# Block-ordered q columns and normalised tiles in an adaLN block of linear attention and a bilinear FFN

## The chip, the cores and the metric

The kernel runs on one core of one Trainium2 chip. The metric is the device time of one execution in microseconds (us). Before the change it was run three times; the median is 558.22 us (558.07 to 559.64).

## The reference

The input is x (2048 tokens by 512), a condition vector c and weights, all float32. c gives six vectors of 512 (shifts, scales, gates). The block is two steps with residuals:

```
mod = silu(c) @ w_mod                      # sa, ca, ga, sb, cb, gb
h = layernorm(x) * (1 + ca) + sa
q, k, v = split(h @ wqkv)                  # 32 heads of 16
pq, pk = phi(q), phi(k)                    # phi(t) = (t + 1 if t > 0 else exp(t)) + 1e-6
o = pq @ (pk.T @ v) / (pq . sum(pk) + 1e-6)     # per head
x = x + ga * (o @ wo)
h = layernorm(x) * (1 + cb) + sb
x = x + gb * (((h @ w_gate) * (h @ w_up)) @ w_down)   # inner width 1376
```

## The kernel before, in words

**Precision.** Every float32 matrix is split into a high part (a copy rounded to fp32r) and a low part (the rest). A product is three matmuls, high x high, high x low and low x high. In `split` (L195) ScalarE (ACT) makes the high part and VectorE (DVE) or GpSimd (POOL) the low part.

**Tiles.** The 2048 tokens are 16 tiles of 128, in four chunks of four. A buffer is 128 x 512 float32 from one pool of 94; PSUM has four banks of the pool ps_acc and four of ps_w.

**First stage (to about 140 us).** Chunk by chunk tokens are normalised (class `Norm`, `xhat` L256), turned on TensorE (PE) and modulated; k products (`proj`, L304), phi, and the sums of keys times normalised tokens in four banks. In iteration i == 2 of this loop the q weights are split (L517). The q products of tiles 0 to 5 are made in the loop, those of tiles 6 to 15 after it. `zb` (L558) holds the sum of keys for the denominators.

**Second stage (about 140 to 275 us).** `wp` is the product of the key-value sums with wo, four high/low pairs. For each tile phi(q) is divided by its denominator (`den_p`, `den_b`, `den_c`), transposed and multiplied by wp on top of x in PSUM (`y_seed` L740, `y_a` L748); `y_b` (L757) takes the bank back to x, and for the last chunk DVE makes the statistics from the bank. `y_step` (L766) is one tile of this. Tiles 0 to 7 are transposed on PE. Tiles 8 to 15 (FLIPPED) are transposed otherwise: `move_out` writes the tile to DRAM, `move_in` fetches it with 32-row blocks exchanged between partitions, and `turn_v` (L719) lets a DVE transpose turn the 32 x 32 blocks; `turn_h` and `turn_l` make the high and low parts. The DVE transpose reads every fourth word (`"p (m i s) -> p m s i"`), so the row order of what it gives is (partition, k) and not (k, partition); for these tiles a second copy of wp in that order is needed: `wp_store` (L691) writes wp to DRAM, `wp_fetch` (L698) reads it back as `wp4`.

**Third stage (about 265 us to the end).** The FFN's columns are taken in groups of 128 (`fts`). Three groups (`lone`) are done plainly for chunks 0 and 1 (`gate_up`, `down`), beside the second stage. The others go through `block` (L1044), a scheme of seven half products instead of eight over pairs of chunks: the left side (class `Left`) has sums s1 to s4 of the normalised, transposed tokens, the right side (class `Right`, L980) sums t1 to t4 of gate and up weights, each split into high and low. `Right.sums` makes the t, `Right.high` and `Right.lows` the parts; helpers `right_load`, `right_sums`, `right_split` (L1133 to L1144). A block has the points p1, p5, p6, p2, p7, p3, p4; each is six matmuls (`times`, L1021) into one of four banks a, b, c, d, and between them ACT copies banks (`copy`, L1031): after p1 bank a is copied into b, and p6 adds to b. `fill(n)` advances the blocks by n points.

The tokens of chunks 2 and 3 reach the blocks without PE: `stow` (L882) writes the normalised tile to DRAM, `unstow` reads it back, `flip` (L894) is a DVE transpose into `wide`, reading every fourth word, and `flipped` (L899) applies scale and shift on ACT, reading `wide` in runs of 32 words. Their row order is again (partition, k). So the gate and up weights for these chunks are loaded in that order (`wg_4`, `wu_4`), and scale and shift are turned by `by_fours` (L875, four small DMAs through DRAM).

**What sets the order.** The program is a schedule written by hand (`manual_schedule`): each engine executes its instructions in the order in which the code records them, and the code from L1203 on fixes how the second stage, the lone groups and the first block interleave. All DMAs are issued by SyncE (SP), in order. Waits between engines follow from the tiles; a buffer of the pool waits for its last user.

The stretch that the change reorders is L1279 to L1346. Two lines of it:

```
    y_step(14, seed=None)      # L1336: the matmuls of tile 14
    fill(1)                    # L1337: p1 of the first block
```

Of the kernel before, what the change touches and what calls it, by code (L numbers as in the profile page):

```python
# [14 lines left out]
P = 128  # L15
# [9 lines left out]
def tile_adaln_block(  # L25
# [33 lines left out]
    wg_4 = w_gate.rearrange("(p k) f -> p k f", p=P)  # L59
    wu_4 = w_up.rearrange("(p k) f -> p k f", p=P)  # L60
# [152 lines left out]
    def cut(pair, a, b):  # L213
        return pair[0][:, a:b], pair[1][:, a:b]


    class Norm:
        def __init__(self, tiles):
# [37 lines left out]
        def xhat(self, *js):  # L256
            for j in js:
                self.n[j] = B("n")
                nc.scalar.activation(self.n[j], self.tiles[j], AF.Identity,  # L259
                                     scale=self.rstd[:, j:j + 1], bias=self.nmr[:, j:j + 1])  # L260

        def xhat_on(self, engine, *js):
# [238 lines left out]
    for i in range(NT):  # L501
        ch, j = divmod(i, NJ)
        done = 0
        if i > 2:
            ahead[i + 2] = proj(i + 2, wk) if i + 2 < NT else proj(i + 6 - NT, wq)
        if i in q_at:
            qps = proj(q_at[i], wq)
        def turn_x():
            to, *ks = turn_at[i]
            nx.transpose(*ks)  # L510
            nx.modulated(ca, sa, *ks, cast=nc.vector)
            norm[to:] = [nx]
# [24 lines left out]
        if ch + 2 < NCH and j == 3:  # L537
            nx = nx2
            nx.stats(2, 3)
            nx.rstd_of()  # L540
            nx.nmr_of()
            nx.xhat(0, 1)
        if i + 2 < NT:
            k_phi(i + 2, ahead.pop(i + 2))
        else:
            q_a(i + 6 - NT, ahead.pop(i + 2))
            q_b(i + 6 - NT)
        if i in q_at:
            q_a(q_at[i], qps)
            q_b(q_at[i])  # L550
        if i + 1 < NT:
            z_add(i + 1)
        if i == NT - 2:
            pairs["z"] = split_raw(zacc, low=nc.gpsimd)
        if i == NT - 1:
            zps = row_sum(pairs["z"])
            zb = consts.tile([P, D], F32, name="zb")
            nc.scalar.activation(zb, zps, AF.Identity, bias=eps_z)  # L558
        t_tile(i, *range(done, KD))
        if i in extra:  # L560
            extra[i]()
# [4 lines left out]

    pzs = {}
    den0 = consts.tile([P, NH], F32, name="den0")

    def den_z():  # L570

        nc.vector.reduce_sum(den0, zb.rearrange("p (h i) -> p h i", i=DH), axis=AX.X)
        nc.vector.tensor_scalar(den0, den0, EPS_PHI, EPS_DEN, op0=ALU.mult, op1=ALU.add)

    def den_p(ch, *js, on=None):
        for j in js:
            pzs[ch, j] = B("f")
            (on or nc.gpsimd).tensor_tensor(pzs[ch, j], phq[ch * NJ + j], zb, op=ALU.mult)

    def den_r(ch, *js):  # L580
        if ch not in dens:
# [8 lines left out]
            den_r(ch, j)  # L590

    def den_b(ch):
        nc.vector.tensor_tensor(dens[ch], dens[ch], den0.unsqueeze(1).to_broadcast([P, NJ, NH]), op=ALU.add)
        nc.vector.reciprocal(dens[ch], dens[ch])

    def den_c(*tiles):
# [87 lines left out]
        turn_h(i)  # L684
        turn_l(i)

    FLIPPED = range(8, NT)
    SUMS = (0, 1, 2)
    wp4, moved = [], {}

    def wp_store():  # L691
        to = [tc.dram_tile([D, D], F32, name=f"wp_{part}") for part in range(2)]
        for g in range(KD):
            for part in range(2):
                nc.sync.dma_start(to[part][g * P:(g + 1) * P], f32(wp[g][part]))
        wp4.append(to)

    def wp_fetch():  # L698
        rows = [x.rearrange("(p k) d -> p k d", k=KD) for x in wp4.pop()]
        for k in range(KD):  # L700
            wp4.append((B("w", dt=F32R), B("w", dt=F32R)))
            for part in range(2):
                nc.sync.dma_start(f32(wp4[k][part]), rows[part][:, k])

    def move_out(*tiles):

# [12 lines left out]
    def turn_v(i):  # L719

        tps[i] = B("f")
        nc.vector.transpose(tps[i].rearrange("p (s m i) -> p m s i", m=NQ, i=BL),
                            moved.pop(i).rearrange("p (m i s) -> p m s i", m=NQ, i=BL))

    def turned_v(i):
        turn_v(i)
# [21 lines left out]
    def y_a(i):  # L748
        if i not in yps:
            y_seed(i)  # L750
        pq = pqs.pop(i)
        for k in range(KD):
            (ah, al), (bh, bl) = cut(pq, k * P, (k + 1) * P), (wp4 if i in FLIPPED else wp)[k]
            for x, y in ((ah, bh), (ah, bl), (al, bh)):
                nc.tensor.matmul(yps[i], x, y, start=False, stop=k == KD - 1 and x is al, skip_group_check=True)  # L755

# [115 lines left out]
        norm2[ch].nmr_of()  # L872
        ln2_xhat(ch)

    def by_fours(col, name):  # L875

        t, v = consts.tile([P, KD], F32, name=name), tc.dram_tile([D], F32, name=name + "_row")
        nc.sync.dma_start(v.rearrange("(k p) -> p k", p=P), col)
        nc.sync.dma_start(t, v.rearrange("(p k) -> p k", k=KD))
        return t  # L880

    def stow(ch, *js):  # L882

        for j in js:
# [9 lines left out]
    def flip(ch, *js):  # L894
        for j in js:
            nc.vector.transpose(wide[:, j].rearrange("p (m s i) -> p m s i", m=NQ, i=BL),
                                blocks.pop((ch, j)).rearrange("p (m i s) -> p m s i", m=NQ, i=BL))

    def flipped(ch, *ks):  # L899
        for k in ks:  # L900
            f = B("f")
            nc.scalar.activation(f.rearrange("p (x i) -> p x i", i=BL),
                                 wide.rearrange("p j (m s i) -> p (j m) s i", m=NQ, i=BL)[:, :, k],
                                 AF.Identity, scale=cb4[:, k:k + 1], bias=sb4[:, k:k + 1])
            blocks[ch, "f", k] = f

    stowed, blocks = {}, {}
# [8 lines left out]
    cb4, sb4 = by_fours(cb, "cb4"), by_fours(sb, "sb4")  # L916
    for ch in range(NCH):
        norm2[ch] = Norm(xts[ch])

# [60 lines left out]
    class Right:  # L980


        def __init__(self, f, plain):
            f0, self.n = fts[f]
            self.up, self.low = self.tile("raw"), self.tile("raw")
            for t, kh in ((self.up, 0), (self.low, 1)):
                for i, v in enumerate((wg_v, wu_v) if plain else (wg_4, wu_4)):
                    nc.sync.dma_start(t[:, i], v[:, kh * KH:(kh + 1) * KH, f0:f0 + self.n])

        def tile(self, tag, dt=F32):  # L990
# [141 lines left out]

    def right_load(n):  # L1133
        if n < len(steps):
            rights[n] = Right(steps[n][1], steps[n][0][0] in PLAIN)

    def right_sums(n, on=None):
        if n < len(steps):
# [74 lines left out]
    y_step(0, lambda: den_c(3), lambda: q_b(11))  # L1213
    y_step(1)
    y_step(2, lambda: split_gu(f0, nc.gpsimd))
    y_step(3, lambda: scale_down(f0), wp_store, turn=False, seed=False)
    ps12 = proj(12, wq)
    y_b(3)
    norm2[0].rstd_of()
# [36 lines left out]
    den_c(7)  # L1256
    den_a(2, 2, on=nc.vector)
    g()
    y_step(5, lambda: den_a(2, 3, on=nc.vector), wp_fetch)
# [37 lines left out]
    y_banks += [acc_bank(), acc_bank()]  # L1297
    y_seed(12, y_bank)
    norm2[2].nmr_of()
    norm2[2].xhat(0, 1)  # L1300
    turn_l(12)
    first[0].sum("s1", "s3", on=nc.gpsimd)
    g(lambda: turn_v(13))
    y_seed(13, y_bank)
    norm2[2].xhat(2, 3)
    turn_h(13)
    turn_l(13)
    move_in(14, 15)
# [40 lines left out]
    norm2[3].nmr_of()  # L1349
    unstow(2)  # L1350
    fill(1)
    norm2[3].xhat(0)
    fill(1)
    norm2[3].xhat(1)
    fill(1)
    norm2[3].xhat(2)
    stow(3, 0, 1)
    fill(1)
    norm2[3].xhat(3)
    stow(3, 2)  # L1360
    second = [Left((2, 3), k) for k in range(KH)]

# [52 lines left out]
```

## Time and profile before

| what | value |
|---|---|
| median of three runs | 558.22 us (558.07 to 559.64) |
| the profiled execution | 559.39 us |
| its span, first to last instruction | 557.7 us |
| mean granted TensorE clock | 0.997 |
| POOL busy | 203.0 us (36%) |
| mean DMA rate | 108 GB/s |

The profile is of one execution. A page gives busy shares, the chain of work that ended last, and groups of instructions by line, with count, busy time, mean time of one, idle time ahead of them and what ended it. In the timeline each row has start, duration, engine, line, operation, output and inputs; a bracket gives idle time of the engine before it and who ended it. PE is matmul, PEld weight loading. The end of a matmul in the rows is modelled, and consecutive matmuls overlap in them; the distance between starts gives the pace.

### The profile page before, as it was taken

The page shows a single profiled execution, that of the slowest core. Times are in us where ns is not written, and L with a number is a line of the kernel's source. Part 1 is how long each engine was busy: PE and PEld are TensorE (multiplying, and loading weights), DVE is VectorE, ACT ScalarE, POOL GpSimd, SP SyncE. Part 2 cuts the span into 40 slices and gives each one's busy share as a digit, 9 for nine tenths or more (in the row PEclk, how much of TensorE's full clock was granted, in tenths as well). Part 3 has the DMA queues.
Part 4 walks back from the last instruction along what each step waited for, and adds up shares of the span by engine and source line. Part 5 has one row for each costly group of instructions (what it writes and reads, how often), then busy time and mean ns, then how long its engine had stood idle before and what let it go on. Part 6 is the DMA issues. An engine that isn't in the chain of part 4 may idle for free.

```text
span 557.7 us, 7356 instructions
## 1 busy us (share of the span) xinstructions
PE 550.1 (99%) x2505; PEld 451.3 (81%) x2505; DVE 377.8 (68%) x605; ACT 291.4 (52%) x539; POOL 203.0 (36%) x203
## 2 busy tenths in 40 slices
PE   8999999999999999999899999999999999999997
PEld 6888888888888878878688888887888888888886
DVE  7896968977947886877877587886553544434435
ACT  3695856646477567566683545554444444444110
POOL 2000000101012300055698666566667446446200
PEclk9899999999999999999999999999999999999999
DMA  8900203220532605846435162591335222100004
GB/s 279 384 16 2 75 25 103 101 76 1 155 100 92 188 20 169 264 143 162 132 75 148 42 201 65 188 318 29 113 114 150 59 56 58 56 21 0 1 0 150
DMA packets 59141, 60.39 MB, mean 108 GB/s; under 512 B 8608, under 2 KB 37536, under 8 KB 59104
## 3 DMA queue, kind: packets, MB, share of 16 engines
q1 hardware_dynamic: 59104, 59.93, 34.3%
q8 instruction: 19, 0.31, 0.2%
q14 instruction: 18, 0.15, 0.1%
HBM read 43.65 MB, written 16.26 MB: 107 GB/s over the span
## 4 chain that ended last, share of the span: by engine, by line
PE 92%; DVE 3%; ACT 2%; DMA 1%; issue 1%; SPq 0%; DVEq 0%; ACTq 0%
PE bank L1026 32%; PE acc L1106 6%; PE acc L1107 6%; PE acc L1108 6%; PE acc L755 5%; PE bank L209 5%; PE bank L211 5%; PE bank L210 5%; PE acc L351 3%; PE acc L349 3%; PE acc L350 3%; PE bank L839 2%; PE bank L837 2%; PE bank L838 2%; PE bank L272 2%; DMA x<-in_A_x_dram 1%
## 5 line engine op out<-in xcount | busy, mean ns | idle before, releaser
L1026 PE MATMUL bank<-h,w 128*128 128x512 f32 (+1 forms) x798 | 185.4, 390 | 1.5 <-ACT bank L1031 1.5
L1026 PEld LDWEIGHTS bank<-h,w 128*128 128x128 f32 (+1 forms) x798 | 148.1, 186 | 35.8 <-ACT bank L1031 2.6
L1031 ACT ACTIVATE bank<-bank 128x512 f32<-128x512 f32 (+1 forms) x38 | 22.1, 583 | 137.1 <-PE bank L1026 137.0
L824 DVE TENSOR_TENSOR x<-acc,x 128x512 f32<-128x512 f32 (+1 forms) x73 | 48.4, 681 | 47.4 <-PE acc L1108 47.3
L1012 POOL TENSOR_TENSOR w<-raw,w 128x256 fp32r<-128x256 f32 (+3 forms) x38 | 41.3, 1086 | 95.2 <-ACT w L1005 95.2
L1107 PE MATMUL acc<-w,kh 128*128 128x512 f32 (+2 forms) x154 | 59.6, 387 | 0.0
L1106 PE MATMUL acc<-w,kh 128*128 128x512 f32 (+2 forms) x154 | 59.6, 387 | 0.0
L1108 PE MATMUL acc<-w,kl 128*128 128x512 f32 (+2 forms) x154 | 59.5, 386 | 0.0
L197 POOL TENSOR_TENSOR w<-raw,w 128x512 fp32r<-128x512 f32 (+1 forms) x25 | 36.0, 1442 | 55.3 <-ACT w L196 28.5
L250 POOL TENSOR_TENSOR rstd<-ve,half 128x4 f32<-128x4 f32 (+1 forms) x10 | 10.8, 1080 | 120.7 <-DVE ve L249 68.0
L1012 POOL TENSOR_TENSOR w<-t,w 128x512 fp32r<-128x512 f32 (+1 forms) x38 | 49.3, 1320 | 0.0
L197 DVE TENSOR_TENSOR kl<-u,kh 128x512 fp32r<-128x512 f32 (+1 forms) x38 | 26.4, 733 | 30.2 <-ACT kh L196 30.2
L209 PE MATMUL bank<-w,h 128*128 128x512 f32 x104 | 40.8, 392 | 0.0
L211 PE MATMUL bank<-w,h 128*128 128x512 f32 x104 | 40.5, 390 | 0.0
L210 PE MATMUL bank<-w,h 128*128 128x512 f32 x104 | 40.5, 389 | 0.0
L755 PE MATMUL acc<-w,xh 128*128 128x512 f32 x120 | 37.7, 395 | 0.0
L1106 PEld LDWEIGHTS acc<-w,kh 128*128 128x128 f32 (+1 forms) x154 | 28.9, 188 | 6.0
L1108 PEld LDWEIGHTS acc<-w,kl 128*128 128x128 f32 (+1 forms) x154 | 28.9, 188 | 5.9
L1107 PEld LDWEIGHTS acc<-w,kh 128*128 128x128 f32 (+1 forms) x154 | 28.9, 188 | 5.9
L1085 DVE TENSOR_TENSOR u<-bank,u 128x512 f32<-128x512 f32 (+1 forms) x19 | 13.1, 687 | 28.9 <-PE bank L1026 22.9
L259 ACT ACTIVATE n<-x,nmr,rstd 128x512 f32<-128x512 f32 x30 | 22.9, 804 | 12.2 <-DVE nmr L254 12.2
L196 ACT ACTIVATE w<-raw 128x512 fp32r<-128x512 f32 (+2 forms) x44 | 26.3, 619 | 1.9 <-DVE raw L804 1.0
(206 smaller groups left out, 1125.1 us busy)
## 6 DMA issues: line engine op xcount, KB each, us to landing
raw<-in_w_mod_dram SPq DMA_DIRECT2D x24, 256.0 KB, 3.8
raw<-in_B_w_down_dram SPq DMA_DIRECT2D x20, 256.0 KB, 3.2
raw<-in_B_w_gate_dram SPq DMA_DIRECT2D x36, 128.0 KB, 3.7
raw<-in_B_w_up_dram SPq DMA_DIRECT2D x36, 128.0 KB, 3.6
x<-in_A_x_dram SPq DMA_DIRECT2D x16, 256.0 KB, 5.7
out_dram<-x SPq DMA_DIRECT2D x15, 256.0 KB, 2.6
raw<-in_A_wqkv_dram SPq DMA_DIRECT2D x12, 256.0 KB, 5.4
wp<-w SPq DMA_DIRECT2D x8, 256.0 KB, 3.3
```

Of the source, the lines that this page charges most:

```text
L196: nc.scalar.activation(h, src, AF.Copy)
L197: (low or nc.vector).tensor_tensor(l, src, f32(h), op=ALU.subtract)
L209: nc.tensor.matmul(ps, ah, bh, start=i == 0, stop=False)
L210: nc.tensor.matmul(ps, ah, bl, start=False, stop=False)
L211: nc.tensor.matmul(ps, al, bh, start=False, stop=i == n - 1)
L755: nc.tensor.matmul(yps[i], x, y, start=False, stop=k == KD - 1 and x is al, skip_group_check=True)
L824: nc.vector.tensor_tensor(xt[:, a:b], dn[j][:, a:b], xt[:, a:b], op=ALU.add)
L1012: sub = lambda out, x, y: (on or nc.gpsimd).tensor_tensor(out, x, f32(y), op=ALU.subtract)
L1026: mm = lambda x, y, **kw: nc.tensor.matmul(ps, x[:, k], y, skip_group_check=True, **kw)
L1106: nc.tensor.matmul(ps, hh[:, a:b], dh[:n, c:d], start=i == 0, stop=False)
L1107: nc.tensor.matmul(ps, hh[:, a:b], dl[:n, c:d], start=False, stop=False)
L1108: nc.tensor.matmul(ps, hl[:, a:b], dh[:n, c:d], start=False, stop=i == len(hs) - 1)
```

## The change

The DVE transposes for tiles 8 to 15 and for chunks 2 and 3 now read contiguous runs. For this the columns inside each row are put into block order before: column (s, q, i), with s of 4, q of 4 and i of 32, stands at place (q, s, i). What the transposes give is then in the plain row order (k, partition). It follows that:

- q weights are split into block order; q products of tiles 0 to 7 read them back in row order, those of tiles 8 to 15 come out in block order. Denominators of tiles 8 to 15 use a copy of zb and of den0 in block order.
- The normalised tiles of chunks 2 and 3 are written in block order.
- wp_store, wp_fetch, wp4, by_fours, wg_4 and wu_4 go.
- Beside that, the order at the start of the first block changes: right_sums(0), right_split(0), turn_v(15) with its parts, the splits s3 and right_sums(1) stand earlier, the additions of down(1, (2, 3)) later, and the banks are no longer permuted.

PE executes the same instructions in the same order, as the two programs show. On POOL one copy is added, on DVE one small copy, and on SP 20 DMAs go.

```
+    FLIPPED = range(8, NCH * NJ)
+    def by_block(x):
+        return x.rearrange("p (s q i) -> p q s i", q=NQ, i=BL)
+    def by_row(x):
+        return x.rearrange("p (q s i) -> p s q i", q=NQ, i=BL)
+    def split_blocks(raw):
+        h, l = B("w", dt=F32R), B("w", dt=F32R)
+        view = lambda x: x.rearrange("p (q s i) -> p q s i", q=NQ, i=BL)
+        nc.scalar.activation(view(h), by_block(raw), AF.Copy)
+        nc.vector.tensor_tensor(view(l), by_block(raw), view(f32(h)), op=ALU.subtract)
+        return h, l
...
+        def xhat_blocks(self, *js):
+            for j in js:
+                self.n[j] = B("n")
+                nc.scalar.activation(self.n[j].rearrange("p (q s i) -> p s q i", q=NQ, i=BL),
+                                     self.tiles[j].rearrange("p (s q i) -> p s q i", q=NQ, i=BL), AF.Identity,
...
-        product(ps, [(cut(norm[ch].t[k], j * P, (j + 1) * P), w[k]) for k in range(KD)])
+        rows = w is wq and i not in FLIPPED
+        product(ps.rearrange("p (s q i) -> p s q i", q=NQ, i=BL) if rows else ps,
+                [(cut(norm[ch].t[k], j * P, (j + 1) * P), tuple(by_row(x) for x in w[k]) if rows else w[k])
+                 for k in range(KD)])
...
-            wq.extend(split_raw(r) for r in raw_q)
+            wq.extend(split_blocks(r) for r in raw_q)
...
+            zq = B("z")
+            nc.gpsimd.tensor_copy(zq.rearrange("p (q s i) -> p q s i", q=NQ, i=BL), by_block(zb))
...
+        nc.vector.tensor_copy(den0q.rearrange("p (q s h) -> p q s h", q=NQ, s=KD),
+                              den0.rearrange("p (s q h) -> p q s h", q=NQ, s=KD))
...
         nc.vector.transpose(tps[i].rearrange("p (s m i) -> p m s i", m=NQ, i=BL),
-                            moved.pop(i).rearrange("p (m i s) -> p m s i", m=NQ, i=BL))
+                            moved.pop(i).rearrange("p (m s i) -> p m s i", m=NQ, i=BL))
...
-            (ah, al), (bh, bl) = cut(pq, k * P, (k + 1) * P), (wp4 if i in FLIPPED else wp)[k]
+            (ah, al), (bh, bl) = cut(pq, k * P, (k + 1) * P), wp[k]
...
             nc.vector.transpose(wide[:, j].rearrange("p (m s i) -> p m s i", m=NQ, i=BL),
-                                blocks.pop((ch, j)).rearrange("p (m i s) -> p m s i", m=NQ, i=BL))
+                                blocks.pop((ch, j)).rearrange("p (m s i) -> p m s i", m=NQ, i=BL))
...
-                for i, v in enumerate((wg_v, wu_v) if plain else (wg_4, wu_4)):
+                for i, v in enumerate((wg_v, wu_v)):
...
     g()
+    right_sums(0, nc.vector)
     y_step(11, lambda: move_in(12), turn=False, seed=False)
...
     turn_v(14)
-    take = down(1, (2, 3))
+    down_13 = down(1, (2, 3))
     first[1].sum("s1", "s3", "s2", "s4", on=nc.gpsimd)
+    right_split(0)
     y_seed(14, y_bank)
     turn_h(14)
+    turn_v(15)
+    turn_l(14)
+    turn_h(15)
     first[0].split("s1", "s2")
-    turn_l(14)
+    first[1].split("s1", "s2")
     y_b(13)
+    turn_l(15)
+    for x in first:
+        x.split("s3")
+    right_sums(1, nc.vector)
     y_seed(15, y_bank)
-    right_sums(0, nc.vector)
-    take()
-    first[1].split("s1", "s2")
-    turn_v(15)
     for n in range(4):
         banks.append(bank())
-    banks[:] = [banks[n] for n in (2, 0, 1, 3)]
     turn_bank[0] = acc_bank
-    right_split(0)
     draw_load(0)
...
     y_step(14, seed=None)
     fill(1)
     y_b(14)
-    right_sums(1, nc.vector)
-    first[0].split("s3", "s4")
     fill(1)
-    first[1].split("s3", "s4")
+    for x in first:
+        x.split("s4")
     fill(2)
+    down_13()
     y_step(15)
```

More of the change, by code (lines that the diff above doesn't have):

```diff
@@ L259, in xhat @@
                 nc.scalar.activation(self.n[j], self.tiles[j], AF.Identity,
+                                     scale=self.rstd[:, j:j + 1], bias=self.nmr[:, j:j + 1])
+        def xhat_blocks(self, *js):
[3 more added lines that the diff above has]
+                                     self.tiles[j].rearrange("p (s q i) -> p s q i", q=NQ, i=BL), AF.Identity,
                                      scale=self.rstd[:, j:j + 1], bias=self.nmr[:, j:j + 1])
@@ L568, in tile_adaln_block @@
     den0 = consts.tile([P, NH], F32, name="den0")
+    den0q = consts.tile([P, NH], F32, name="den0q")
     def den_z():
@@ L577, in den_p @@
             pzs[ch, j] = B("f")
[L578 removed]
+            (on or nc.gpsimd).tensor_tensor(pzs[ch, j], phq[ch * NJ + j], zq if ch * NJ + j in FLIPPED else zb, op=ALU.mult)
     def den_r(ch, *js):
@@ L592, in den_b @@
     def den_b(ch):
-        nc.vector.tensor_tensor(dens[ch], dens[ch], den0.unsqueeze(1).to_broadcast([P, NJ, NH]), op=ALU.add)
+        nc.vector.tensor_tensor(dens[ch], dens[ch], (den0q if ch * NJ in FLIPPED else den0).unsqueeze(1).to_broadcast([P, NJ, NH]), op=ALU.add)
         nc.vector.reciprocal(dens[ch], dens[ch])
@@ L685, in turn @@
         turn_l(i)
-    FLIPPED = range(8, NT)
     SUMS = (0, 1, 2)
[L689 to L703, printed above, removed]
+    moved = {}
     def move_out(*tiles):
@@ L873, in ln2_nx @@
         ln2_xhat(ch)
[L875 to L880, printed above, removed]
     def stow(ch, *js):
@@ L980, in tile_adaln_block, with __init__ @@
     class Right:
-        def __init__(self, f, plain):
+        def __init__(self, f):
             f0, self.n = fts[f]
@@ L1134, in right_load @@
         if n < len(steps):
-            rights[n] = Right(steps[n][1], steps[n][0][0] in PLAIN)
+            rights[n] = Right(steps[n][1])
     def right_sums(n, on=None):
@@ L1215, in tile_adaln_block @@
     y_step(2, lambda: split_gu(f0, nc.gpsimd))
-    y_step(3, lambda: scale_down(f0), wp_store, turn=False, seed=False)
+    y_step(3, lambda: scale_down(f0), turn=False, seed=False)
     ps12 = proj(12, wq)
@@ L1258, in tile_adaln_block @@
     g()
-    y_step(5, lambda: den_a(2, 3, on=nc.vector), wp_fetch)
+    y_step(5, lambda: den_a(2, 3, on=nc.vector))
     y_step(6, lambda: den_b(2), lambda: ready(8))
@@ L1299, in tile_adaln_block @@
     norm2[2].nmr_of()
-    norm2[2].xhat(0, 1)
+    norm2[2].xhat_blocks(0, 1)
     turn_l(12)
@@ L1304, in tile_adaln_block @@
     y_seed(13, y_bank)
-    norm2[2].xhat(2, 3)
+    norm2[2].xhat_blocks(2, 3)
     turn_h(13)
@@ L1351, in tile_adaln_block @@
     fill(1)
-    norm2[3].xhat(0)
+    norm2[3].xhat_blocks(0)
     fill(1)
-    norm2[3].xhat(1)
+    norm2[3].xhat_blocks(1)
     fill(1)
-    norm2[3].xhat(2)
+    norm2[3].xhat_blocks(2)
     stow(3, 0, 1)
     fill(1)
-    norm2[3].xhat(3)
+    norm2[3].xhat_blocks(3)
     stow(3, 2)
```

5 lines of the change are left out of this document (1 added, 4 removed).

## The prediction

> **What bounds the kernel now.** I read the page first, then the waits of TensorE (PE), then the chain in order of time, then the timeline around the one wait that counts.
>
> ```profile
> span 557.7 us, 7356 instructions
> PE 550.1 (99%) x2505; PEld 451.3 (81%) x2505; DVE 377.8 (68%) x605; ACT 291.4 (52%) x539; POOL 203.0 (36%) x203
> PE 92%; DVE 3%; ACT 2%; DMA 1%; issue 1%; SPq 0%; DVEq 0%; ACTq 0%
> ```
>
> PE is busy 99% of the span, and 92% of the chain that ended last is PE. So an edit on another engine pays only where PE waits for it, and an edit to the matmuls themselves pays or costs directly. The waits of PE say where it waits:
>
> ```profile
> PE acc L148 <- DVE w L143: 2.0, 1, 2.0
> PE bank L1026 <- ACT bank L1031: 1.5, 1, 1.5
> PE bank L279 <- ACT n L259: 0.4, 1, 0.4
> ```
>
> The first and third belong to the start, which the change doesn't touch. The second is one wait of a block's matmuls (L1026) for a PSUM copy on ACT (L1031). The next rows show its place; the first of them, from the chain, gives PE's undisturbed pace: 9.52 us for 42 matmuls of 512 columns, 0.2267 us each.
>
> ```profile
> 302.69 9.52 PE bank L1026 x42
> ```
>
> ```profile
> 260.86 0.62 PE L755 MATMUL acc<-w,xh 128*128 128x512 f32 x2
> ...
> 263.59 3.19 PE L1026 MATMUL bank<-h,w 128*128 128x512 f32 x12
> 263.70 2.38 DVE L197 TENSOR_TENSOR h<-s,h 128x512 fp32r<-128x512 f32 x2
> 263.73 3.50 POOL L1012 TENSOR_TENSOR w<-t,w 128x512 fp32r<-128x512 f32 x2
> ...
> 266.00 1.08 DVE L722 STREAM_TRANSPOSE f<-u 128x512 f32<-128x512 f32 x1
> 267.12 0.63 ACT L676 ACTIVATE xh<-f 128x512 fp32r<-128x512 f32 x1 [2.61 <-DVE f L722]
> 267.19 1.27 POOL L1012 TENSOR_TENSOR w<-raw,w 128x512 fp32r<-128x512 f32 x1
> 267.66 0.58 ACT L1031 ACTIVATE bank<-bank 128x512 f32<-128x512 f32 x1
> ...
> 268.29 3.02 PE L1026 MATMUL bank<-h,w 128*128 128x512 f32 x12 [1.51 <-ACT bank L1031]
> ...
> 271.15 0.61 PE L755 MATMUL acc<-w,xh 128*128 128x512 f32 x2
> ```
>
> Twelve matmuls from 263.59 (the points p1 and p5 of the first block) would let the next (p6) start at 263.59 + 12 x 0.2267 = 266.31. It starts at 268.29, 1.98 us late. The next twelve should lead to 271.01 and lead to 271.15, 0.14 late. That is **2.1 us** of PE time. Its cause reads backwards: p6 adds into bank b, which ACT copies from bank a (267.66). ACT runs in order, and ahead of the copy stands the high part of tile 15 (L676), which waited 2.61 us for the DVE transpose turn_v(15) (L722, 266.00), which stood behind two low parts of left sums (L197) that took 2.38 us while POOL made the low parts of the first right side.
>
> **The change part by part.** (a) *Order.* PE's instructions keep their order exactly; what moves is on DVE and ACT. right_sums(0), four DVE subtractions, goes ahead of norm2[2].rstd_of.
>
> ```profile
> 240.54 0.69 DVE L197 TENSOR_TENSOR kl<-phi,kh 128x512 fp32r<-128x512 f32 x1 [0.70 <-ACT kh L196]
> 243.35 0.17 DVE L247 TENSOR_SCALAR ve<-sums 128x4 f32<-128x4 f32 x1 [2.11 <-ACT acc L238]
> ```
>
> ```profile
> 230.67 0.40 SPq L988 DMA_DIRECT2D raw<-in_B_w_up_dram  x1
> raw<-in_B_w_up_dram SPq DMA_DIRECT2D x36, 128.0 KB, 3.6
> ```
>
> ```profile
> 261.06 0.39 DVE L994 TENSOR_TENSOR t<-raw 128x256 f32<-128x256 f32 x1
> 262.17 0.42 DVE L994 TENSOR_TENSOR t<-raw,t 128x256 f32<-128x256 f32 x1
> ```
>
> They took 261.06 to 262.59, 1.53 us, and now stand in a hole of 2.11 us between 241.23 and 243.35. Their weights were asked for by 230.67 and land about 3.6 us later, so the new wait on them is over before DVE gets there; if it were not, L247 and the normalisation of chunk 2 would queue behind it.
>
> right_split(0) follows the copy of y 12 on ACT, so POOL can make the low parts as soon as its eight left sums are done; turn_v(15) and its high part now precede all left splits, and four left splits move ahead of y_b(13). I lay the new order out from old rows:
>
> ```profile
> 255.21 0.68 DVE L229 BATCH_NORM_STATS2 st<-acc 128x6 f32<-128x512 f32 x1
> 255.32 1.29 POOL L944 TENSOR_TENSOR s<-f,s 128x512 f32<-128x512 f32 x1
> 256.10 1.10 DVE L722 STREAM_TRANSPOSE f<-u 128x512 f32<-128x512 f32 x1
> 260.96 0.60 ACT L746 ACTIVATE acc<-x 128x512 f32<-128x512 f32 x1 [1.57 <-DVE st L229]
> ```
>
> ```profile
> L1012 POOL TENSOR_TENSOR w<-raw,w 128x256 fp32r<-128x256 f32 x18 | 14.5, 804 | 90.2 <-ACT w L1005 90.2
> ```
>
> DVE is at turn_v(14) at 256.10 as before and, at the old 1.10 each, through turn_v(15) at 258.3. Then come five subtractions (xl of 14, four left lows), the statistics of y 13, seed 15 on ACT (which reuses that bank), and the copy of a into b. POOL has its last sum done at 256.6 and four lows to make, one of half size: 0.80 + 3 x 1.27 = 4.6 us, to 261.2 if alone. ACT makes the high parts and copies y 13 from 258.3 on (five of 0.63, to 261.5, then the copy to 262.1). Without contention DVE's five (0.69 each) follow ACT and end at 262.2. If DVE and POOL took strict turns, DVE's 3.45 and the 2.9 that POOL has left at 258.3 add up to 6.35, to 264.7. The statistics (0.68) then end between 262.9 and 265.4, seed 15 (0.60) between 263.5 and 266.0. The copy (0.58) can't start before p1's last matmul ends: its start 263.59 + 5 x 0.2267 = 264.72, plus 0.39 for one (the 390 ns of L1026 below), 265.1. So the copy ends between 265.7 and 266.6, due at 266.31. I take it as in time: the two L197 beside POOL took 2.38 in place of 1.38, 0.5 more each, and about three of the five meet POOL, so they end at 258.3 + 3.45 + 1.5 = 263.3 and seed 15 at 264.6. The other bound is 0.3 late, plus 0.14 for the restart.
>
> ```profile
> L1026 PE MATMUL bank<-h,w 128*128 128x512 f32 x756 | 175.6, 390 | 1.5 <-ACT bank L1031 1.5
> L680 DVE TENSOR_TENSOR xl<-f,xh 128x512 fp32r<-128x512 f32 x8 | 7.7, 965 | 4.3 <-ACT xh L676 4.1
> L680 DVE TENSOR_TENSOR xl<-bank,xh 128x512 fp32r<-128x512 f32 x8 | 5.5, 688 | 4.2 <-ACT xh L676 4.2
> ```
>
> The same subtraction takes 688 ns with one input in PSUM and 965 with both in SBUF, where POOL works beside it. The Trainium skill, SBUF — State Buffer, section "Who interferes with whom", says that a DVE instruction with two SBUF inputs and a reading GpSimd instruction hold one lock, and the loser blocks fully; these two rows agree. By that rule the strict turns, with 0.4 us of the gain lost, would be the end; it is part of the first rival.
>
> The second left parts' other moves have room: with p6 at 266.31 the third point that needs s3 and t3 (p7) comes after two more groups of six and the twelve of tile 15, at 266.31 + 24 x 0.2267 = 271.75; s3's lows and right_sums(1) (1.53) follow the statistics on DVE and are through by about 268.5. The adds of down_13 (two of 0.68) move behind them; nobody takes those two banks before the first down_group. SP's draw_load(1) now waits for POOL's last right low and delays right_load(2) by some 2 us; these weights are used a block later.
>
> (b) *Contiguous flips.* Sixteen DVE transposes read runs instead of every fourth word.
>
> ```profile
> L722 DVE STREAM_TRANSPOSE f<-u 128x512 f32<-128x512 f32 x8 | 8.8, 1097 | 0.0
> L896 DVE STREAM_TRANSPOSE wide<-u 128x512 f32<-128x512 f32 x8 | 8.6, 1088 | 0.0
> L902 ACT ACTIVATE f<-wide,sb,cb 128x512 f32<-128x512 f32 x8 | 6.4, 806 | 0.7 <-DVE wide L896 0.7
> L259 ACT ACTIVATE n<-x,nmr,rstd 128x512 f32<-128x512 f32 x30 | 22.9, 804 | 12.2 <-DVE nmr L254 12.2
> ```
>
> They would fall from about 1.09 us towards the 0.69 of a plain DVE pass, at most 0.4 each; two of them lie in the chain above, but the layout already holds with 1.10, so I book nothing. The flips of chunks 2 and 3 lie beside blocks with DVE less than full. xhat_blocks and split_blocks use runs of 32 words on ACT or DVE: L902 reads just such runs and takes 806 ns against 804 for the contiguous L259, so I price them at nothing; at the most 0.4 us a DVE pass (the price of L722's words).
>
> ```profile
> 40.13 2.49 DVE L197 TENSOR_TENSOR w<-raw,w 128x512 fp32r<-128x512 f32 x4
> 44.25 0.39 PE L209 MATMUL bank<-w,h 128*128 128x512 f32 x1
> 132.02 2.49 DVE L197 TENSOR_TENSOR w<-n,w 128x512 fp32r<-128x512 f32 x4
> 135.07 0.22 PE L209 MATMUL bank<-w,w 128*128 128x128 f32 x1
> ```
>
> Four split lows end at 42.6 and PE first reads wq at 44.25: 1.6 us of cover, just what 4 x 0.4 would use. The added zq copy (POOL, about one 1.29 us pass) and den0q (a 128x32 DVE pass, 0.2) delay DVE's w<-n by at most 1.5 us; they end at 134.5, PE starts on them at 135.07 with the first and needs the last later: covered within about 0.1 us.
>
> (c) *PE reads q weights by rows.* For tiles 0 to 7, 8 x 12 = 96 matmuls read their moving side in 16 runs of 32 words. PE writes the same contiguous bank. No matmul of this trace does that. Nearest rows: L902, the same runs on another engine, +2 ns; L722, words instead of runs, 1097 against 688, x1.6, which would be 0.136 us each, 13 us in all. I take nothing, because L902 has the same geometry; below nothing is excluded, since the same number of columns passes. The Trainium skill, Advanced Engine Details and Errata, section "Memory Cachelines", says that SBUF reads within one 16-byte line go at full rate, which these runs satisfy, but also, of PSUM, that non-contiguous patterns slow matmuls; no run yet shows which holds here.
>
> (d) *Removed.* Sixteen 256 KB transfers of wp and four column transfers leave SP. PE waits for none of them, so nothing.
>
> **Sum:** -2.1 (stall), 0 for the rest: the profiled execution of 559.39 us (span 557.7 and 1.7 around it) would be 557.3. It lies 0.2% over the median of the runs; the median 558.22 less 2.1 is 556.1, and I forecast **556.2**, 0.1 being left for an incomplete restart.
>
> **The rivals.** *A new wait takes part of the old one's place*: seed 15 and the copy come late, by strict turns of DVE and POOL (0.4 us: 556.5 to 556.6; 10%), or because tile 15's block or a sum arrives later than laid out (up to all 2.1 us: 558.2; 14%). For it: a copy that starts at 265.1 has only 0.6 us to spare. Against: seed 15 has 0.5 us in front of that start.
>
> *PE reads runs slower* (the other side): place, the 96 matmuls of (c). At 21 ns each (9%) the gain is used up, at 39 ns the kernel is slower by 0.3%; at L722's ratio it ends at 556.1 + 13 = 569. For it: 128-byte hops are new to PE, which has no slack at all. Against: L902. 18%, with the smaller mishaps of that side.
>
> That the flips don't become faster (the price being that of writing runs) changes nothing here, as the layout used 1.10.
>
> **How the numbers follow.** 0.3% of 558.22 is 1.67 us, about what a measurement can tell from no change. Forecast 58%: 555.6 to 556.5, faster. First rival 10% + 14% = 24%: 556.5 to 558.2, within 0.3%. Second rival 18%: from 558.4 up to 569; the range takes the first two whole and the edge of the third: 555.5 to 558.5. Faster 0.58, same 0.24, slower 0.18.
>
> **What would show it.** Right: no PE wait on the bank copy, the block's first 24 matmuls without a break, and all later times 2 us earlier. Transposes near 0.7 us confirm (b).
>
> ```profile
> 155.65 2.75 PE acc L755 x12
> ```
>
> If the q products of tiles 0 to 7 take more than 0.227 us a matmul, so that tile 0's output product (L755) starts later than 155.65, (c) is wrong. If PE waits at p6 again, look whether DVE's statistics or POOL's lows ended last.

## The result and the profile after

The changed kernel takes 557.41 us (median of 10 runs, 557.13 to 558.21); the kernel before, run beside it, 558.76 us (10 runs, 558.07 to 561.21). The ratio is 0.9967, 95% interval 0.9952 to 0.9982: 1.8 us faster by the ratio (1.0 to 2.7), 1.35 by the medians. The ratio compares means, and four of the ten runs of the kernel before took 559.64 to 561.21 us, which the median hardly feels. The profiled execution took 557.53 us. In later runs, on other occasions, the same kernel gave 557.33 us against 558.9, ratio 0.9966 (0.9954 to 0.9978).

The page of the changed kernel, the same lines as those shown of before (span, busy time, chain by engine):

```profile
span 555.8 us, 7319 instructions
PE 549.9 (99%) x2505; PEld 451.2 (81%) x2505; DVE 371.4 (67%) x606; ACT 291.4 (52%) x539; POOL 204.1 (37%) x204
PE 99%; DVE 0%; issue 0%
```

PE was 92% of the chain before and is 99% of it now: ahead of the first block the old chain ran over ACT, DVE and a transfer from 238 to 268 us, and the new one stays on PE. Its waits (engine, line waited at, releaser: total us, times, longest):

```profile
PE acc L146 <- DVE w L141: 2.0, 1, 2.0
```

The wait on the bank copy is gone; the 2.0 us at the start, which the change doesn't touch, are left. (The small wait of 0.4 us at the start is absent from this execution and there again in the next one of the same kernel.) The timeline shows the place of the old stall:

```profile
255.81 1.31 DVE L736 STREAM_TRANSPOSE f<-u 128x512 f32<-128x512 f32 x2
...
257.54 3.45 POOL L1018 TENSOR_TENSOR w<-t,w 128x512 fp32r<-128x512 f32 x2
...
258.34 5.50 DVE L195 TENSOR_TENSOR h<-s,h 128x512 fp32r<-128x512 f32 x4 [0.21 <-ACT h L194]
...
260.95 1.73 POOL L1018 TENSOR_TENSOR w<-raw,w 128x512 fp32r<-128x512 f32 x1
...
263.69 5.60 PE L1032 MATMUL bank<-h,w 128*128 128x512 f32 x24
263.76 0.69 DVE L242 BATCH_NORM_STATS2 st<-acc 128x6 f32<-128x512 f32 x1
...
264.48 0.60 ACT L760 ACTIVATE acc<-x 128x512 f32<-128x512 f32 x1 [3.09 <-DVE st L242]
...
265.25 0.58 ACT L1037 ACTIVATE bank<-bank 128x512 f32<-128x512 f32 x1 [0.17 <-PE bank L1032]
```

Before, there were two rows of 12 matmuls with 1.51 us of idle time between; now the block's first 24 matmuls are one row. Both transposes are through by 257.1, and the copy starts at 265.25 behind PE itself (0.17 us of ACT idle, ended by p1's last matmul), no longer behind ACT's high part of tile 15.

The groups of the transposes, and of the operations that now write or read in block order (count, busy us, mean ns):

```profile
L736 DVE STREAM_TRANSPOSE f<-u 128x512 f32<-128x512 f32 x8 | 5.5, 700 | 0.0
L903 DVE STREAM_TRANSPOSE wide<-u 128x512 f32<-128x512 f32 x8 | 5.5, 699 | 0.0
L279 ACT ACTIVATE n<-x,nmr,rstd 128x512 f32<-128x512 f32 x8 | 6.2, 804 | 0.0
L225 ACT ACTIVATE w<-raw 128x512 fp32r<-128x512 f32 x4 | 2.2, 626 | 0.0
```

The transposes fall from 1097 and 1088 ns to 700 and 699. The block-ordered normalisation (L279, 804) costs what the plain one did, the block-ordered high part of the q weights (L225, 626) what a plain one does.

What came back is on PE. One q product, tile 0, in the view of a line's matmuls: L209 of the kernel before, then L207 of the changed one. One line issues every third matmul of the twelve; the columns are duration min/median/max in ns and the first and last start.

```profile
L209 PE MATMUL bank<-w,h x4: 389/389/389, 44.2 to 46.3; 128*128 128x512 f32 x4
```

```profile
L207 PE MATMUL bank<-w,h x4: 395/396/396, 43.6 to 45.7; 128*128 128x512 f32 x4
```

The modelled duration follows the pace (it is the distance of two starts plus 0.163 us), so 389 to 396 says that each matmul comes 7 ns later. The starts themselves lie 226.6 ns apart before and 233.3 after, 6.7 ns more. It is so in seven of the tiles 0 to 7 and in no other product; tile 4 starts unevenly in both kernels (its second matmul comes 0.32 us after its first) and differs by 18 ns in all. Summed over the eight tiles the starts give 0.58 us, against 96 x 6.7 ns = 0.64 us if tile 4 paid in full. A stall of 2.1 us gone, 0.58 us spent: 1.5 us net, inside the interval.

The loss also shows at the place that the prediction named, the start of tile 0's output product, but only as a distance: from the first q matmul of tile 0 to the first matmul of that product it is 111.16 us before and 111.84 after. By the time from the program's start (155.41 and 155.44) nothing would be seen, because this execution of the changed kernel reached its first q matmul 0.65 us sooner. Kernels with the same code up to there reached it between 43.38 us (right_only) and 44.55 us (order_only), and the change can't be why.

### The profile page after: what moved, and what is told of

It is laid out like the page before. It is cut to its first block, busy times and chain, and to the rows that moved or that the text cites. A ratio compares the mean times of both kernels' runs of the same rounds, so it can differ in the third digit from the quotient of the medians.

```text
span 555.8 us, 7319 instructions
## 1 busy us (share of the span) xinstructions
PE 549.9 (99%) x2505; PEld 451.2 (81%) x2505; DVE 371.4 (67%) x606; ACT 291.4 (52%) x539; POOL 204.1 (37%) x204
## 4 chain that ended last, share of the span: by engine, by line
PE 99%; DVE 0%; issue 0%
PE bank L1032 33%; PE acc L769 7%; PE acc L1113 6%; PE acc L1112 6%; PE acc L1114 6%; PE bank L207 5%; PE bank L209 5%; PE bank L208 5%; PE acc L375 3%; PE acc L374 3%; PE acc L373 3%; PE bank L853 2%; PE acc L146 2%; PE bank L851 2%; PE bank L852 2%; PE bank L293 2%
## 5 line engine op out<-in xcount | busy, mean ns | idle before, releaser
L207 PE MATMUL bank<-w,h 128*128 128x512 f32 x104 | 41.0, 394 | 0.0
L209 PE MATMUL bank<-w,h 128*128 128x512 f32 x104 | 40.7, 392 | 0.0
L1000 POOL TENSOR_TENSOR t<-raw,t 128x256 f32<-128x256 f32 (+1 forms) x34 | 25.9, 761 | 1.3
L769 PEld LDWEIGHTS acc<-w,xh 128*128 128x128 f32 x120 | 22.0, 188 | 4.4
```

The costliest lines, as they stand in the source:

```text
L207: nc.tensor.matmul(ps, ah, bh, start=i == 0, stop=False)
L209: nc.tensor.matmul(ps, al, bh, start=False, stop=i == n - 1)
L1000: sub = lambda out, x, y: (on or nc.gpsimd).tensor_tensor(out, x, y, op=ALU.subtract)
```

## The experiments

Theory A: the new order takes the 2.1 us away, and PE's reading in runs costs 0.6 us. Rival B: the runs are free and the layout (shorter transposes, fewer transfers) earns part of the gain. All ratios are to the kernel before, run beside each.

| kernel | median, us | ratio (95%) |
|---|---|---|
| again (the changed kernel) | 557.33 | 0.9966 (0.9954 to 0.9978) |
| order_only | 556.40 | 0.9946 (0.9928 to 0.9964) |
| order_again (the same) | 556.70 | 0.9955 (0.9938 to 0.9973) |
| layout_only | 559.33 | 0.9998 (0.9986 to 1.0010) |
| copied | 556.69 | 0.9948 (0.9930 to 0.9966) |
| doubled | 558.05 | 0.9977 (0.9965 to 0.9990) |
| turn_only | 559.04 | 0.9997 (0.9985 to 1.0009) |
| right_only | 558.29 | 0.9988 (0.9977 to 1.0000) |
| runs, patterns (one execution each) | 559.29, 564.76 | |

**again**, the changed kernel once more:

> The changed kernel unaltered, for a comparison on one chip. Theory A: the new order takes 2.1 us of PE waiting away and the q products of tiles 0 to 7, which read runs, give 0.64 us back (96 x 6.7 ns), so -1.5 us against before (ratio 0.9973). Rival B: the reading of runs costs nothing and the whole is the first measurement's ratio, -1.8 us or more (0.9967).

It repeats the result. The ratio is the rival's 0.9967 rather than theory A's 0.9973, but its interval holds both, so this run doesn't decide between them; the runs that follow do.

**order_only**: the kernel before with the change's new order of the stretch and nothing else.

```
+    right_sums(0, nc.vector)      # ahead of y_step(11)
...
+    right_split(0)                # behind first[1].sum
...
+    turn_v(15)
+    turn_l(14)                    # was behind first[0].split
+    turn_h(15)
...                                # and the rest of that hunk
```

> The kernel before with the new order at the first block alone; flips, wp round trip and q columns as before. Theory A: PE's wait is gone although the transposes still take 1.10 us, -2.1 us against before (ratio 0.9962), 0.6 us below the changed kernel, and all q matmuls start 226.7 ns apart. Rival B: the shorter transposes are needed for the copy of bank a into b to be in time, so a PE wait of 0.3 us or more remains at p6 and the kernel lies above the changed one.

The whole gain is here, with the slow transposes and all transfers still in place: 0.9946, and 0.9955 when it was repeated. By the medians it is the fastest of these kernels, 0.9 us below the changed one (556.40 against 557.33; 0.6 when repeated). The intervals of the ratios overlap, so that it beats the changed kernel rests on PE's starts as well: its q matmuls lie 226.7 ns apart, and from the first of them to tile 0's output product it is 111.28 us, against 111.84 and 111.87 in the two profiles of the changed kernel. PE runs through the stretch in one piece; the chain of order_only in order of time (start, us, what):

```profile
264.18 5.44 PE bank L1026 x24
269.62 2.72 PE acc L755 x12
```

**layout_only**: the changed kernel with that hunk put back to the old order.

> The changed kernel with the order of before: contiguous flips, q columns by block, no wp round trip, old order at the first block. Theory A: one transpose 0.4 us shorter is ahead of the late copy, so the PE wait falls from 2.1 to about 1.7 us, and the q products cost 0.64 more: +0.2 us against before, no difference. Rival B: flips and 20 fewer DMAs bring something of their own, the kernel is 0.5 us or more below before.

No gain: 0.9998. Its waits of PE, and then its chain through the stretch:

```profile
PE bank L1032 <- ACT bank L1037: 0.6, 1, 0.6
PE bank L1032 <- DVE u L1091: 0.2, 1, 0.2
```

```profile
262.37 0.68 DVE x L838
263.05 2.29 DVE h L195 x2
265.34 0.63 DVE f L736
...
266.66 1.62 DVE xl L709
...
270.49 3.01 DVE h L195 x4
273.49 1.70 DVE raw L1177
275.19 0.61 DVE u L1091
...
275.84 2.33 PE bank L1032 x9
```

The shorter transposes do shorten the old stall: the wait on the copy is 0.6 us where it was 1.5. But the chain stays on DVE until 275.8 and a second, small wait opens there; PE's lost time between 260 and 280 us (starts of matmuls against their undisturbed pace) falls only from 2.15 to 1.48 us. Those 0.67 us are used up by the 0.58 us of the runs. So the layout is worth something only where the order is bad; with the new order, and with PE reading the runs, it is only a cost.

**copied**: the changed kernel, but the q weights are split in plain order and used so for tiles 0 to 7; block-ordered copies are made later for tiles 8 to 15. PE reads no runs.

```
-            wq.extend(split_blocks(r) for r in raw_q)
+            wq.extend(split_raw(r) for r in raw_q)
...
+    wqb.extend(blocks_of(x) for x in wq)   # ACT high parts, POOL low parts
```

> The changed kernel, but q weights are split in row order as before and copied into block order (high parts on ACT, low parts on POOL) once tiles 0 to 7 are done, so that every q product reads contiguous columns. Theory A: the 0.64 us come back, 0.6 us below the changed kernel, -2.1 us against before. Rival B: same time as the changed kernel. If the eight copies come late for tile 8, PE waits ahead of its product at 141 us and the gain is lost.

0.9948: 0.64 us less than the changed kernel by the medians (556.69 against 557.33; the intervals overlap), and the pace is back; from the first q matmul to tile 0's output product it is 111.20 us:

```profile
L207 PE MATMUL bank<-w,h x5: 389/389/389, 42.3 to 45.0; 128*128 128x512 f32 x5
```

copied has no second copy of wp and 16 transfers of 256 KB less than order_only, and stands where that stands. So the transfers and the transposes are worth nothing that these runs can tell.

**doubled**: the suspected cost alone, twice. order_only, to which only this is added: q weights in block order, and the q products of all 16 tiles read them back in row order.

```
+        rows = w is wq
+        product(ps.rearrange("p (s q i) -> p s q i", q=NQ, i=BL) if rows else ps,
+                [(cut(...), tuple(by_row(x) for x in w[k]) if rows else w[k]) ...
...
+            wq.extend(split_blocks(r) for r in raw_q)
```

> The new order on the old layout, to which only the suspected cost is added, twice over: q weights are split into block order and the q products of all 16 tiles, not 8, read them back in row order; the transposes, the second copy of the product weights and all transfers stay as before. Theory (reading in runs costs 6.7 ns in each of the matmuls): 192 x 6.7 = 1.3 us over the order alone, and where that one stands at a ratio of 0.995 (0.9946 and 0.9955), this stands at 0.9973; the q products' starts lie 233.3 ns apart in all tiles. Rival (the runs are free, and the changed kernel stands above the order alone for another reason, such as the transposes or the transfers): 0.995, and 226.7 ns.

Ratio 0.9977 for 0.9973 expected, 0.0022 to 0.0031 over the order alone, which is 1.2 to 1.7 us for 1.3. A tile after the eighth, read contiguously in order_again and in runs in doubled, shows it (L210 of each):

```profile
L210 PE MATMUL bank<-w,h x4: 389/389/389, 144.0 to 146.1; 128*128 128x512 f32 x4
```

```profile
L210 PE MATMUL bank<-w,h x4: 396/396/397, 144.7 to 146.8; 128*128 128x512 f32 x4
```

Its starts lie 233.3 ns apart, against 226.6 contiguously, and 233.2 to 233.4 in all tiles that nothing else holds up; over the 16 tiles the starts add up to 1.1 us more than in order_again. The interval of the ratio overlaps that of order_again, so the price itself rests on these starts, and the ratio agrees. One more wait of 0.4 us (on DVE, L1101) stands in the profiled execution of doubled, so not all of the difference need be the runs.

**turn_only** and **right_only**: which half of the new order does it? The first is the kernel before with turn_v(15) moved right behind turn_v(14). The second is the kernel before with only right_sums(0) ahead of y_step(11) and right_split(0) behind first[1].sum.

```
     turn_v(14)
+    turn_v(15)              # turn_only
...
-    turn_v(15)
```

```
+    right_sums(0, nc.vector)   # right_only: ahead of y_step(11)
...
+    right_split(0)             # behind first[1].sum
```

> The kernel before with one line moved: the transpose of tile 15 stands right behind that of tile 14. Theory (the transpose behind the crowd on DVE is what the bank copy waits for): the copy is in time and the wait on it goes. What is late next is the last low part of the first right side on POOL, which ends at 268.46 in the kernel before and is read by the point after p6, due at 267.67: a wait of 0.8 us on POOL takes part of the place, so about 2.1 - 0.85 = 1.25 us are gained, ratio 0.9978. Rival (the whole new order is needed, the copy being held by something else too): PE still waits 1 us or more for the copy, ratio 0.9985 or more.

> The kernel before with only the first right side earlier: its four DVE sums ahead of tile 11's output step, its split right behind the recording of the last left sums; tile 15's transpose stays at its old, late place. Theory (the crowd): without 1.53 us of sums and about 1 us of contention with POOL ahead of it, the transpose ends 2.5 us sooner, about 264.8, the copy ends about 266.0, in time for 266.31, and the wait goes whole: 2.1 us gained, ratio 0.9962. Rival (the place of the transpose alone decides): PE still waits 1 us or more for the copy, ratio 0.998 or more.

> The new order alone on the old layout, as in order_only, beside the two halves of that order: if the halves each take the wait away, the three lie within 1 us of each other, order_again lowest at a ratio of 0.995 to 0.9965.

Both theories miss in both kernels. In turn_only the wait on the copy goes, as the theory said; in right_only it shrinks to 0.06 us of idle time (0.33 us by the starts). In each another wait takes its place. The waits of PE in turn_only, and in right_only:

```profile
PE bank L1026 <- DVE u L1085: 1.1, 1, 1.1
PE bank L1026 <- POOL w L1012: 0.4, 1, 0.4
```

```profile
PE acc L755 <- DVE xl L680: 1.1, 1, 1.1
```

turn_only gains nothing (0.9997). The expected wait on POOL's last low part is there, 0.4 us instead of 0.8, but behind it DVE, which has the same work left in the same stretch, comes too late to the addition (L1085) that has to read a bank of the block before PE adds to it again. Its chain:

```profile
263.08 2.30 DVE h L197 x2
265.39 1.70 DVE xl L680
...
269.57 4.13 DVE h L197 x4
273.70 1.30 DVE raw L1171
...
275.32 0.69 DVE u L1085
...
276.05 4.15 PE bank L1026 x17
```

right_only (0.9988) moves POOL's low parts to where DVE makes the parts of tile 14, and these become late instead (DVE, then PE, in the timeline):

```profile
257.68 2.39 DVE L197 TENSOR_TENSOR h<-s,h 128x512 fp32r<-128x512 f32 x2 [1.22 <-ACT h L196]
260.00 1.76 DVE L680 TENSOR_TENSOR xl<-f,xh 128x512 fp32r<-128x512 f32 x1
```

```profile
261.82 0.50 PE L755 MATMUL acc<-w,xl 128*128 128x512 f32 x1 [1.09 <-DVE xl L680]
```

Moving one instruction out of the way only shows the next. The stall was not one late instruction but a stretch in which DVE, with POOL on the same memory, had more to do than fitted; the whole order does several things at once. right_sums(0) (1.53 us on DVE) and the additions of down_13 (1.28 us, at 262.50 in the kernel before, at 270.44 in the changed one) leave the stretch, tile 15's transpose stands early, and tile 14's low part stands ahead of the left lows that POOL slows down. Which of these are needed beyond the two halves tried here was not separated.

**runs** and **patterns**: what sets the price of PE's reading? Each tile from 0 to 7 reads its 12 x 512 words in another pattern.

```
+        run = 128 >> i                                  # runs
+        x.rearrange("p (a b i) -> p b a i", a=2, i=run)
...
+        a, run = ((4, 64), (4, 16), (4, 8), (4, 1), (2, 1), (2, 2), (8, 1), (256, 1))[i]   # patterns
```

> The changed kernel, but the q products of tiles 0 to 7 read their weights in runs that get shorter from tile to tile: 128 words for tile 0, then 64, 32, 16, 8, 4, 2 and 1 word for tile 7 (4, 8, 16, ... 512 runs in a row of 512). The columns of q of these eight tiles come out in another order, so their tokens' output is not the reference's. Price per run (6.7 ns for 16 runs, so 0.42 ns each): the starts of a tile's matmuls lie 226.6 ns plus 1.7, 3.3, 6.7, 13, 27, 53, 107 and 213 apart. Price per pattern (any third dimension costs 6.7 ns): 233.3 in all eight tiles. Price per memory line of four words (the Trainium skill, Advanced Engine Details and Errata, section Memory Cachelines, by which reads inside one 16-byte line go at full rate): no more than 233.3 down to runs of four words, and a step at two words (tile 6) and another at one (tile 7). The whole kernel by the price per run is about 12 x 0.426 = 5.1 us longer than without any runs, some 4.4 us over the changed kernel.

> After the kernel with runs of 128 words down to one, whose tiles lay 226.7, 226.7, 236.4, 240.1, 243, 250, 340 and 216 ns a matmul apart, none of the three prices stands. Here the q products of tiles 0 to 7 read eight other patterns of the same 512 words (columns in another order, so the output of these tokens is not the reference's): runs of 64, 16, 8 and 1 words taken from four quarters in turn (tiles 0 to 3), runs of 1 and 2 words from two halves (tiles 4 and 5, as before), single words from eight parts (tile 6), every second word (tile 7). If the number of runs and not the distance of the jump sets the pace: 226.7 for tile 0, 240 for tile 1, 243 for tile 2, 216 for tiles 3, 4, 6 and 7, 340 for tile 5. If the jump counts, tiles 1, 2, 3 and 6 differ from that by more than 5 ns. If 216 for single words was a slip of one tile's place and not of the pattern, tiles 3, 4, 6 and 7 lie at 227 or above.

Distance of the starts in ns, mean over a tile's matmuls but the first (contiguous: 226.6); the row for 4 parts and runs of 32 is the changed kernel's:

| taken in turn from | 128 words | 64 | 32 | 16 | 8 | 4 | 2 | 1 |
|---|---|---|---|---|---|---|---|---|
| 2 halves | 226.7 | 226.7 | 236.6 | 240.5 | 243.3 | 251.1 | 339.6 | 215.8 |
| 4 parts | | 226.6 | 233.3 | 232.6 | 230.7 | | | 280.7 |
| 8 parts | | | | | | | | 488.9 |
| 256 parts (every second word) | | | | | | | | 451.0 |

Four rows of these, from the views of line L207: tiles 1 and 2 of runs (64 and 32 words), then tiles 4 and 6 of patterns (single words from 2 and from 8 parts):

```profile
L207 PE MATMUL bank<-w,h x4: 389/389/389, 52.1 to 54.2; 128*128 128x512 f32 x4
L207 PE MATMUL bank<-w,h x4: 398/399/402, 67.7 to 69.8; 128*128 128x512 f32 x4
```

```profile
L207 PE MATMUL bank<-w,h x4: 379/380/462, 118.3 to 120.4; 128*128 128x512 f32 x4
L207 PE MATMUL bank<-w,h x4: 667/667/721, 131.0 to 135.5; 128*128 128x512 f32 x4
```

The price per run falls: 8 runs of 64 words are free, and from 4 parts 64 runs of 8 cost no more than 16 of 32. The price per pattern falls too (-11 to 262 ns). The same runs cost something else from 4 parts than from 2 (233.3 against 236.6 for 16 runs of 32): the distance of the jump counts or the number of parts, which these kernels change together. The price by memory lines fits in part: runs of four words or more cost 0 to 25 ns, one or two words up to 262. But single words from two halves are the fastest of all, 215.8, and the step at two words was not followed by another at one. The kernel of runs as a whole took 559.29 us, 1.9 over the changed kernel's median where the price per run gave 4.4. Which rule gives these numbers stays open, and each rests on one execution; what is settled is the price of the pattern in the kernel, 6.7 ns.

## Why the prediction was right, and where a term was off

Forecast 556.2 (555.5 to 558.5), measured 557.41. Of the 1.2 us between, 0.54 is the reference: the sum started from the three runs' median of 558.22, and the kernel before, run beside the changed one, has 558.76. The rest is one term, 0.58 us: 556.2 + 0.54 + 0.58 = 557.3. That this comes within 0.1 us is partly luck: the runs tell the gain only to 1.0 to 2.7 us.

- **The stall and its cause: right.** 2.1 us of PE's time were named with their chain (transpose, high part, copy). PE's lost time between 260 and 280 us falls from 2.15 to 0.03 us in the changed kernel and to 0.03 in order_only. Not all of it was the copy: 0.28 us were lost ahead of p6, at the matmul of 265.59, which starts 0.05 us after POOL's first large low part ends (265.54); the list of waits doesn't show it, since the modelled end of the matmul before covers it. turn_only, where POOL's lows stay late, still loses these 0.28 us; the new order, which makes them earlier, doesn't. What the prediction did not see is that either half of the new order alone gains nothing or little; its layout of all of DVE's, ACT's and POOL's instructions was the step that the simpler stories lack.
- **The layout of the stretch: in time as forecast, but by errors that offset each other.** The five subtractions were put at 263.3 by "about three of the five meet POOL", 0.5 us more each, with strict turns at 264.7 as the other end. They ended at 263.84. Four met a low part of POOL: tile 14's took 0.84 us and the next three 1.50, 1.78 and 1.77, against 0.69 alone; the last, after POOL was done (262.68), took 0.68. Two rows show it:

```profile
261.46 1.77 DVE L195 TENSOR_TENSOR h<-s,h 128x512 fp32r<-128x512 f32 x1
263.16 0.68 DVE L195 TENSOR_TENSOR h<-s,h 128x512 fp32r<-128x512 f32 x1
```

That is 3.1 us of contention where 1.5 were assumed; the five began at 257.30 and not at 258.3, which took 1.0 of the extra 1.6 back. POOL's full-size lows took 1.73 to 1.75 us beside them instead of 1.27, so one of each took 1.7 to 1.8 us, near the 1.96 (0.69 + 1.27) of strict turns. This agrees in the main with the Trainium skill, SBUF — State Buffer, section "Who interferes with whom", by which the two engines exclude each other from the ports that they share. Seed 15 ended at 265.08 instead of 264.6, and the copy's 0.5 us of room shrank to 0.17, yet it was in time, and the first rival's 0.4 us of loss did not come. Nor did the shorter transposes decide it. In order_only, which has the long ones, the five begin 0.9 us later, counted from p1, but two of them and not one come after POOL is done; the contention is 2.1 us, and in both kernels the statistics start 0.07 us after p1. The sooner start only made DVE meet POOL for longer.

- **right_sums(0) in DVE's hole: right.** It ran from 241.26 to 242.81, and no wait on its weights appeared.
- **Shorter transposes: right in size** (0.39 to 0.40 us each), and at nothing in the sum; layout_only shows what the layout is worth in the old order: 0.67 us of stall.
- **Runs on ACT and DVE, zq and den0q: right,** nothing; DVE's block-ordered low parts of the q weights took 0.68 us each, as the plain ones.
- **Transfers removed: right,** nothing: order_only, which keeps them, is not slower.
- **PE reads q weights by rows: the term that was mis-sized.** "I take nothing, because L902 has the same geometry" put the term at 0 between bounds of 0 and 13 us; it measured 6.7 ns a matmul, 0.58 us in all, more than a quarter of the stall's 2.1. L902 reads on ACT, and its 806 against 804 ns said nothing of PE, which takes a column in 0.44 ns where ACT takes 1.6 (226.6 and 804 ns for 512); that PE's speed is why it notices the runs was not tried. Nor does "below nothing is excluded, since the same number of columns passes" hold in general: single words from two halves go below the contiguous pace, if not in this kernel. The second rival was this mechanism, with the point of no gain at 21 ns; 6.7 is a third of that. The Trainium skill, Advanced Engine Details and Errata, section "Memory Cachelines", has full speed while accesses stay in one 16-byte line and a penalty where each goes to another; 16 runs of 32 words stay in a line four words at a time, yet cost 3%, and single words from two halves, each in another line than the one ahead of it, take 215.8 ns, less than the contiguous read: the measurement decides.

## What to carry to other kernels

When a bound engine stalls, don't price the move of the one instruction that the wait names: lay out everything that the crowded engines have in that stretch, since here one half of a reorder gained nothing (0.9997), the other little (0.9988), each passing the stall on, and the whole removed it (0.9946). A change of layout should be made where an engine has room; the price of a strided read on one engine is no estimate for another, least of all for the one at 99%. Here the order alone, or the order with block-ordered copies made off the bound engine, lies below both kernels by the medians; against the changed one this is 0.6 to 0.9 us, in line with PE's starts.

## What the runs showed of the hardware that was not expected

- A matmul of 512 fp32r columns whose moving side comes in 16 runs of 32 words takes 6.7 ns (4 parts) or 10 ns (2 halves) more than its 226.6; in runs of 64 or 128 words nothing more; words one by one 215.8 to 488.9.
- A DVE transpose of 128 x 512 words takes 1097 ns when it reads every fourth word and 700 when it reads runs, while the block-ordered passes on ACT (804 and 626 ns) and DVE (684 ns) cost nothing extra.
- A subtraction on DVE that alternates with POOL's took 1.77 to 1.78 us against 0.69 alone, and POOL's 1.74 against 1.27; starting DVE's earlier only made more of them meet POOL.
